# Fused attention, channel mix and gated feed-forward on one core: four more heads without a split, wider first loads, and new planner numbers

## The chip, the cores and the metric

The kernel runs on one NeuronCore of a Trainium2 chip. The metric is device time in microseconds (us) of one execution; lower is better. Engines go by short names: PE is TensorE (PEld its weight loads), DVE is VectorE, ACT is ScalarE, POOL is GpSimd, SP is SyncE, which issues nearly all the DMA transfers here.

## The reference

Three blocks follow each other in float32 on a batch of 4 with 576 positions: block-causal attention (8 heads of 64), a channel mix with a feed-forward (512 to 1024 to 512), and a gated feed-forward with a product over positions.

```python
scores = scale * np.matmul(q, k.transpose(0, 1, 3, 2))
mask = (pos[:, None] // 64) >= (pos[None, :] // 64)
attn = softmax(np.where(mask, scores, -1e9))
x = (attn @ v)                      # heads side by side: (4, 576, 512)

xk = mu_k * x + (1.0 - mu_k) * x_prev        # x_prev: one position earlier
xr = mu_r * x + (1.0 - mu_r) * x_prev
k = np.maximum(xk @ w_k, 0.0)
x = sigmoid(xr @ w_r) * (k * k @ w_v)

h = gelu(x @ w_in); u, v = split(h)
v_s = einsum('ts,bsd->btd', w_sg, layernorm(v) * g_ln) + b_sg
out = x + (u * v_s) @ w_out
```

## The kernel before

**Two ways to multiply in float32.** PE multiplies plain float32 in two passes at half the column rate of the type `float32r`, which holds fewer digits. Most products are therefore made of pairs: an operand is split into a high part and the rest (`xh`/`xl`, `kh`/`kl`, `PH`/`PL`, `K`/`k2`), and two or three `float32r` products are added up in PSUM. The split costs work on ACT (the rounding copy), POOL and DVE (the subtraction). A direct product takes plain float32 and needs no split.

**Attention.** The unit of work is one batch, one head and one kind: `LO` has the queries 0 to 319, `HI` the queries 320 to 575 with all 576 keys. There are 64 units; the first 16 are `LO` of batches 0 and 1, the next 16 `HI` of the same batches. Units with a number under `DIRECT = 16` are direct: their q and k come by one transfer of 66 rows (64 of the head, two that carry the mask) into `t[0:66]`, their v by another. A unit makes scores (`emit_S`, into the PSUM tiles `SA`, `SB`, or `M` for two early ones), the row maxima on DVE (`stats`), exponentials on ACT (`P`), transposes on PE (`emit_T`, into `T`), a copy of these out of PSUM (`PH` or `PL` for direct units, both for split ones), and the product with v (`emit_PV`, `direct_PV`, into `O`). A direct unit's output stands with the queries as rows, and PE transposes it once more for each pair of heads (`otmp`).

**Feed-forwards.** From the first four pairs of heads on, the mixed inputs (`mix`, tiles `t`, `xh`, `xl`) go into products of 288 columns with the weights, in PSUM tile `M`. The weights come as float64 words and are turned into `float32r` pairs by a chain over ACT, DVE and POOL (`w_split`, tiles `u`, `th`, `w`). The later attention units are spread between these products. The gated feed-forward of all four batches follows from about 440 us on.

**The planner.** The kernel first records every operation, and `Plan.play` then plays them through a table of costs and latencies: the next operation on an engine is the ripe one with the least rank. The order so found is written out as the program. `takes` holds the costs, `Gate` a model of PE's clock with two levels, `MB`, `CB`, `XV` and others shift ranks. Where the planner sees PE stand still it writes fillers, which multiply a tile of zeros (`calm`): 128 columns wide, or, while an output in `O` is open, zeros added into that output (`zeros`). A filler changes no result.

## Time and profile before

| | |
|---|---|
| median of 3 runs | 702.46 us (701.78 to 705.37) |
| profiled execution | 702.29 us |
| its span, first to last instruction | 700.6 us |
| PE busy, share of the span | 691.2 us, 99% |
| DVE, ACT, POOL busy | 467.8, 462.7, 326.9 us (67%, 66%, 47%) |

The span lies inside the execution's own time; 1.7 us of it are outside. Busy time of PE counts overlapping matmuls as one stretch, so that 99% doesn't mean that PE works at its peak. All of the kernel's operations go through one helper, so that every row has the same source line (L586, in the change L596), and the tiles tell the rows apart.

### The profile page before, as it was taken

To read this page: it belongs to the slowest core of one execution; us is meant where nothing else is said; L and a number is where in the kernel's file an instruction comes from. 1 tells how busy PE (TensorE), PEld (TensorE's weight loads), DVE (VectorE), ACT (ScalarE), POOL (GpSimd) and SP (SyncE) were. 2 spreads that over 40 slices of the span, in tenths; PEclk is the share of its full clock that TensorE was granted. 3 is DMA by queue.
4 is the path that set the end of the run, shared out by engine and by line. 5 is a ranking of instruction groups with operands and counts; after the bars stand their busy time and mean duration, and the time that the engine had idled before them with its cause. 6 is when DMAs were issued, how large, how long until landed. Compare 5 with 4: busy or idle time off the path is not lost.

```text
span 700.6 us, 13886 instructions
## 1 busy us (share of the span) xinstructions
PE 691.2 (99%) x4953; PEld 661.9 (94%) x4953; DVE 467.8 (67%) x1169; ACT 462.7 (66%) x1301; POOL 326.9 (47%) x386
## 2 busy tenths in 40 slices
PE   8999999999999999999999999999999999999998
PEld 7888899998999999999999999999899998998998
DVE  3887656877877776775777886773899256346223
ACT  5767898898899899899799889682552132032120
POOL 4634657566566667567557654340334032022031
PEclk9999999999999999999999999999999999999999
DMA  8852126423322332433323310721900400400102
GB/s 256 345 143 64 36 69 197 139 76 110 102 70 84 109 105 68 140 90 111 104 85 96 111 59 16 251 78 52 356 14 1 137 1 0 136 1 9 61 1 68
DMA packets 34565, 69.21 MB, mean 99 GB/s; under 512 B 6048, under 2 KB 20384, under 8 KB 34496
## 3 DMA queue, kind: packets, MB, share of 16 engines
q1 hardware_dynamic: 34352, 68.32, 30.7%
q8 instruction: 39, 0.64, 0.4%
q14 instruction: 30, 0.25, 0.1%
q10 hardware_dynamic: 144, 0.00, 0.0%
HBM read 55.47 MB, written 9.44 MB: 93 GB/s over the span
## 4 chain that ended last, share of the span: by engine, by line
PE 87%; ACT 7%; DVE 2%; DMA 2%; issue 1%; POOL 1%; ACTq 0%; POOLq 0%
PE M L586 43%; PE O L586 17%; PE T L586 11%; PE V L586 7%; PE SA L586 5%; PE SB L586 5%; ACT P L586 2%; DMA q<-Q 1%; ACT PH L586 1%; ACT R L586 1%; ACT otmp L586 1%; ACT t L586 1%; ACT K L586 0%; ACT kh L586 0%; ACT Q L586 0%
## 5 line engine op out<-in xcount | busy, mean ns | idle before, releaser
L586 PE MATMUL M<-xh,w 128*128 128x288 f32 x688 | 163.6, 305 | 0.6 <-ACT xh L586 0.3
L586 PEld LDWEIGHTS M<-xh,w 128*128 128x128 f32 x688 | 117.5, 189 | 1.8 <-ACT xh L586 0.6
L586 PE MATMUL M<-xl,w 128*128 128x288 f32 x344 | 102.5, 299 | 0.0
L586 PE MATMUL M<-kh,w 128*128 128x288 f32 x416 | 97.7, 302 | 0.0
L586 PE MATMUL T<-ident,P 128*128 128x128 f32 x480 | 79.0, 287 | 1.3 <-ACT P L586 0.6
L586 POOL TENSOR_TENSOR gt<-gt,U 128x288 f32<-128x288 f32 x32 | 30.2, 946 | 102.4 <-DVE gt L586 51.4
L586 POOL TENSOR_TENSOR xl<-t,xh 128x288 fp32r<-128x288 f32 x64 | 53.7, 839 | 50.1 <-ACT xh L586 50.0
L586 DVE TENSOR_TENSOR PL<-T,PH 128x256 fp32r<-128x256 f32 (+3 forms) x128 | 68.4, 545 | 11.7 <-ACT PH L586 10.2
L586 ACT ACTIVATE PH<-T 128x384 fp32r<-128x384 f32 (+4 forms) x144 | 65.8, 480 | 9.1 <-PE T L586 8.5
L586 PEld LDWEIGHTS M<-kh,w 128*128 128x128 f32 x416 | 70.6, 188 | 0.0
L586 PEld LDWEIGHTS T<-ident,P 128*128 128x128 f32 x480 | 61.1, 149 | 6.5 <-DVE PL L586 1.9
L586 POOL TENSOR_TENSOR kl<-R,kh 128x288 fp32r<-128x288 f32 x64 | 54.0, 848 | 27.1 <-ACT kh L586 24.8
L586 PEld LDWEIGHTS M<-xl,w 128*128 128x128 f32 x344 | 65.1, 189 | 0.1
L586 DVE TENSOR_SCALAR_CACHE_REDUCE P<-P,rr 128x448 f32<-128x448 f32 (+3 forms) x112 | 63.9, 594 | 0.9
L586 POOL TENSOR_TENSOR k<-qkv,K 64x576 fp32r<-64x576 f32 (+1 forms) x48 | 60.3, 1256 | 5.0 <-ACT K L586 2.3
L586 PE MATMUL M<-kl,w 128*128 128x288 f32 x208 | 61.6, 296 | 0.0
L586 ACT ACTIVATE U<-M 128x288 f32<-128x288 f32 x32 | 13.2, 411 | 71.8 <-PE M L586 71.8
L586 POOL TENSOR_TENSOR V<-qkv,V 128x320 fp32r<-128x320 f32 (+1 forms) x48 | 38.1, 793 | 32.7 <-ACT V L586 22.3
L586 POOL TENSOR_TENSOR Q<-qkv,Q 64x256 fp32r<-64x256 f32 (+1 forms) x48 | 37.9, 790 | 32.1 <-PE SB L586 12.0
L586 PE MATMUL O<-gh,w 128*128 128x288 f32 x256 | 52.0, 295 | 0.1
L586 PE MATMUL O<-PL,V 128*128 128x256 f32 (+2 forms) x208 | 51.6, 284 | 0.3 <-DVE PL L586 0.3
L586 PE MATMUL O<-PH,V 128*128 128x256 f32 (+2 forms) x208 | 51.9, 279 | 0.0
(186 smaller groups left out, 1938.3 us busy)
## 6 DMA issues: line engine op xcount, KB each, us to landing
qkv<-qkv_hi_dram SPq DMA_DIRECT2D x32, 576.0 KB, 3.8
qkv<-qkv_lo_dram SPq DMA_DIRECT2D x16, 416.0 KB, 3.6
x2d<-th SPq DMA_DIRECT2D x32, 144.0 KB, 2.9
X<-x2d SPq DMA_DIRECT2D x4, 1152.0 KB
outT_dram<-o SPq DMA_DIRECT2D x32, 144.0 KB, 1.8
w<-w_k_dram SPq DMA_DIRECT2D x8, 512.0 KB, 7.7
w<-w_v_dram SPq DMA_DIRECT2D x8, 512.0 KB, 9.0
w<-w_in_dram SPq DMA_DIRECT2D x8, 512.0 KB, 8.3
```

What stands on the lines that cost most here:

```text
L586: getattr(getattr(self.nc, e), fn)(*pos, **{k: real(x) for k, x in a.items() if k[0] != "_"})
```

## The change

`DIRECT` goes from 16 to 20: units 16 to 19, the first four `HI` units (heads 0 to 3 of batch 0), become direct, with q, k and mask rows from a new input `later`. The inputs `first` and `later` get 128 rows of which the last 62 are zeros, and the first `PADDED = 4` units load and multiply all 128. The transfer of v loses 64 columns of zeros. In the planner, transposes and products get other costs, a matmul may not start before its weights could be loaded behind the matmul ahead (`preload`, `began`), and seven constants change.

```diff
-BACKLOG = 8000
+BACKLOG = 6000
-FILL_DUTY = 0.7
+FILL_DUTY = 1.0
+COOL = 0.44
...
-            self.slow = u < (HOT if self.slow else 0.38)
+            self.slow = u < (HOT if self.slow else COOL)
...
+def preload(fn, a):
+
+    if fn == "transpose":
+        return 100.0
+    return (220.0 if a["lhsT"].tile.dt == F32 else 109.0) * (1.0 if a["lhsT"].cols > 64 else 0.51)
...
                     gap = t - free[e]
+                    s = t = max(t, began + preload(op.alts[i][1], op.alts[i][2]) * (2.0 if gate.slow else 1.0))
...
-MB = 0
-CB = -500
+MB = -300
+CB = -200
...
-DIRECT = 16
+DIRECT = 20
+PADDED = 4
...
-            nc.sync.dma_start(out=t[0:66, 0:nq + nk], in_=first[b, h])
-            nc.sync.dma_start(out=t[:, nq + nk:nq + nk + nv + 64], in_=src[:, nq + nk:nq + nk + nv + 64])
-            splits[n] = (t[0:66, 0:nq], t[0:66, nq:nq + nk], None)
-            vs[n] = t[:, nq + nk:nq + nk + nv + 64]
+            r = 128 if n < PADDED else 66
+            nc.sync.dma_start(out=t[0:r, 0:nq + nk], in_=(later if kind else first)[b, h, 0:r])
+            nc.sync.dma_start(out=t[:, nq + nk:nq + nk + nv], in_=src[:, nq + nk:nq + nk + nv])
+            splits[n] = (t[0:r, 0:nq], t[0:r, nq:nq + nk], None)
+            vs[n] = t[:, nq + nk:nq + nk + nv]
...
-        for c in CHUNKS[LO]:
+        pe(sum(c + 1 for c in CHUNKS[kind]) * 220.0)
+        chunks = CHUNKS[kind]
+        N = len(chunks)
+        for i, c in enumerate(chunks):
             for j in range(c + 1):
-                u, src = next((u, o) for u, (ts, _) in enumerate(GROUPS[LO]) for tj, tc, o in ts if (tj, tc) == (j, c))
-                mm(ot[:, 64 * c:64 * c + 64], trans[n, u][0][:, src:src + 128], V[:, 64 * j:64 * j + 64],
+                u, src = next((u, o) for u, (ts, _) in enumerate(GROUPS[kind]) for tj, tc, o in ts if (tj, tc) == (j, c))
+                mm(ot[:, 64 * i:64 * i + 64], trans[n, u][0][:, src:src + 128], V[:, 64 * j:64 * j + 64],
                    start=j == 0, stop=j == c)
...
+    def direct(q0, q1, *blocks):
+
+
+        qk = np.concatenate([i[n][0:2].swapaxes(2, 3)[..., lo:q1] for n, lo in (("q", q0), ("k", 0))], axis=-1)
+        rows = np.zeros_like(qk)
         for r, s in enumerate(blocks):
-            rows[..., r, s:s + 64] = 1.0
-            rows[..., r, q1 + s + 64:q1 + s + 128] = -2.0 ** 33
+            rows[..., r, s - q0:s - q0 + 64] = 1.0
+            rows[..., r, q1 - q0 + s + 64:q1 - q0 + s + 128] = -2.0 ** 33
         return c(np.concatenate([qk, rows], axis=-2))
...
+        "first": direct(0, 320, 64, 192),
+        "later": direct(320, S, 320, 448),
```

How the change moves instructions is shown at three places. The first is the start of PE's program, with the scores of units 0 to 2 and the transposes of unit 0. The tiles `kh` and `kl` hold the loads of the first four units at this point (two in each). Before:

```order
L586 MATMUL O<-calm 64x128 x15
L586 MATMUL SA<-kh 64x64
L586 MATMUL SA<-kh 128x192
L586 MATMUL SB<-kh 128x320
L586 MATMUL M<-kh 64x64
L586 MATMUL M<-kh 128x192
L586 MATMUL M<-kh 128x320
L586 MATMUL T_159<-ident,P_88 128x128 x3
L586 MATMUL T_170<-ident,P_88 128x128 x3
L586 MATMUL SB<-kl 64x64
L586 MATMUL SB<-kl 128x192
L586 MATMUL SA<-kl 128x320
```

With the change:

```order
L596 MATMUL O<-calm 64x128 x18
L596 MATMUL SA<-kh 64x64
L596 MATMUL SA<-kh 128x192
L596 MATMUL SB<-kh 128x320
L596 MATMUL M<-kh 64x64
L596 MATMUL M<-kh 128x192
L596 MATMUL M<-kh 128x320
L596 MATMUL SB<-kl 64x64
L596 MATMUL SB<-kl 128x192
L596 MATMUL T_165<-ident,P_88 128x128 x2
L596 MATMUL T_173<-ident,P_88 128x128
L596 MATMUL SA<-kl 128x320
```

Two pieces of the third unit's scores now stand ahead of the first unit's transposes, and three fillers are added.

The second place is DVE at the same time: row maxima (`stats`), the first outputs (`otmp`) and the weight chain (`u`, `th`). Before:

```order
L586 TENSOR_REDUCE stats<-SA 128x1
L586 TENSOR_SCALAR u<-u 128x512
L586 TENSOR_REDUCE rr<-sums 128x3
L586 TENSOR_SCALAR u<-u 128x512
L586 TENSOR_TENSOR otmp<-O,rr 128x3x64
L586 SCALAR_TENSOR_TENSOR u<-w,u 128x512
L586 RECIPROCAL rr<-rr 128x3
L586 SCALAR_TENSOR_TENSOR u<-w,u 128x512
L586 TENSOR_SCALAR u<-u 128x512
L586 TENSOR_REDUCE stats<-M 64x1
L586 TENSOR_SCALAR u<-u 128x512
L586 TENSOR_REDUCE stats<-M 128x1 x2
```

With the change:

```order
L596 TENSOR_REDUCE stats<-SA 128x1
L596 TENSOR_REDUCE stats<-M 64x1
L596 TENSOR_REDUCE stats<-M 128x1
L596 TENSOR_REDUCE rr<-sums 128x3
L596 RECIPROCAL rr<-rr 128x3
L596 TENSOR_TENSOR otmp<-O,rr 128x3x64
L596 TENSOR_REDUCE rr<-sums 128x3
L596 RECIPROCAL rr<-rr 128x3
L596 TENSOR_REDUCE stats<-M 128x1
L596 TENSOR_SCALAR u<-u 128x512 x2
L596 TENSOR_TENSOR otmp<-O,rr 128x3x64
L596 SCALAR_TENSOR_TENSOR u<-w,u 128x512
```

The maxima of the fourth unit (`stats<-M`) now come ahead of the whole weight chain; ahead of them stood two of its steps `u<-w,u` and four `u<-u`, now none.

The third place is one `HI` unit on PE, its product with v and the next unit's scores. Before, split (the letters `k`, `q` are the second pair):

```order
L586 MATMUL O<-PH_1374,V 128x256
L586 MATMUL O<-PL_1384,V 128x256
L586 MATMUL SA<-K,Q 128x448
L586 MATMUL SA<-k_145,q_161 128x448
L586 MATMUL O<-PH_1378,V 128x256
L586 MATMUL O<-PL_1397,V 128x256
L586 MATMUL O<-PH_1378,V 128x256
L586 MATMUL O<-PL_1397,V 128x256
L586 MATMUL O<-PH_1404,V 128x128
```

With the change, direct:

```order
L596 MATMUL O<-calm 64x128 x8
L596 MATMUL O<-qkv,PH_1443 128x64
L596 MATMUL O<-qkv,PH_1478 128x64 x2
L596 MATMUL O<-qkv,PH_1495 128x64
L596 MATMUL O<-qkv,PH_1443 128x64
L596 MATMUL O<-qkv,PH_1478 128x64 x2
L596 MATMUL O<-qkv,PH_1495 128x64
L596 MATMUL SA<-qkv 128x448
L596 MATMUL M<-kh,w 128x288
L596 MATMUL M<-kl,w 128x288
```

Ten `float32r` products of up to 256 columns with v become nine plain ones of 64 columns, and six pieces of scores become three plain ones.

## Rows read from the trace of the kernel before

**Rows 1.** The page: busy time of PE, and its granted clock in 40 slices.

```profile
PE 691.2 (99%) x4953; PEld 661.9 (94%) x4953; DVE 467.8 (67%) x1169; ACT 462.7 (66%) x1301; POOL 326.9 (47%) x386
...
PEclk9999999999999999999999999999999999999999
```

**Rows 2.** Busy time by stage: window, length, engines, PEclk, DMA share, GB/s.

```profile
0.00:49.00 49.00, 47.24 (x192) 39.65 (x192) 34.28 (x86) 32.08 (x93) 24.04 (x41) 1.00 0.76 254
49.00:76.50 27.50, 26.07 (x216) 22.09 (x216) 20.61 (x58) 19.14 (x59) 11.11 (x10) 1.00 0.24 74
76.50:130.00 53.50, 52.86 (x391) 49.70 (x391) 33.82 (x88) 47.59 (x146) 36.30 (x37) 1.00 0.37 109
76.50:440.00 363.50, 360.61 (x2770) 352.12 (x2770) 265.18 (x726) 328.63 (x980) 230.74 (x267) 1.00 0.32 95
```

**Rows 3.** Timeline of PE ahead of 50 us: start, length, engine, tiles, form, number.

```profile
1.18 1.86 PE L586 MATMUL O<-calm 128*64 128x128 f32 x15 [1.18 <-POOL calm L586]
3.62 1.42 PE L586 MATMUL SA<-kh 66*64 66x64 f32 x4 [0.57 <-DMA kh<-first_dram]
...
36.30 1.27 PE L586 MATMUL SA<-qkv 66*128 66x320 f32 x2
37.37 0.85 PE L586 MATMUL T<-ident,P 128*128 128x128 f32 x3
...
42.08 2.67 PE L586 MATMUL O<-qkv,PH 128*128 128x64 f32 x12
44.54 0.85 PE L586 MATMUL T<-ident,P 128*128 128x128 f32 x3
...
47.94 2.00 PE L586 MATMUL O<-qkv,PL 128*128 128x64 f32 x12
```

**Rows 4.** The same view behind 57 us.

```profile
60.49 0.85 PE L586 MATMUL SB<-qkv 66*64 66x64 f32 x4
61.18 0.70 PE L586 MATMUL SA<-qkv 66*128 66x320 f32 x2
61.72 0.28 PE L586 MATMUL T<-ident,P 128*128 128x128 f32 x1
...
76.48 0.38 PE L586 MATMUL M<-xh,w 128*128 128x288 f32 x1
...
85.38 1.45 PE L586 MATMUL O<-qkv,PH 128*128 128x64 f32 x12
86.64 0.38 PE L586 MATMUL M<-xh,w 128*128 128x288 f32 x1
```

**Rows 5.** The same view of split HI units: transposes, scores, product with v.

```profile
141.45 0.82 PE L586 MATMUL T<-ident,P 128*128 128x128 f32 x6
...
144.16 0.37 PE L586 MATMUL SA<-K,Q 128*128 128x448 f32 x1
...
145.09 0.30 PE L586 MATMUL M<-xh,w 128*128 128x288 f32 x1
...
145.90 0.28 PE L586 MATMUL O<-PH,V 128*128 128x256 f32 x1
...
147.08 0.29 PE L586 MATMUL M<-xh,w 128*128 128x288 f32 x1
```

**Rows 6.** Busy time by window: fillers (calm) alone, then all up to unit 10's maxima.

```profile
49.00:76.50 27.50, 5.75 (x77) 5.15 (x77) 0.00 (x0) 0.00 (x0) 1.00 0.24 74
...
0.00:69.25 69.25, 66.52 (x360) 56.19 (x361) 49.34 (x127) 45.31 (x134) 32.31 (x48) 1.00 0.62 204
```

**Rows 7.** Groups of 100 to 440 us: busy us, mean ns of one, idle before.

```profile
L586 ACT ACTIVATE K<-qkv 128x576 fp32r<-128x576 f32 x32 | 21.7, 679 | 0.0
...
L586 ACT ACTIVATE V<-qkv 128x320 fp32r<-128x320 f32 x32 | 15.0, 470 | 0.1
...
L586 ACT ACTIVATE Q<-qkv 128x256 fp32r<-128x256 f32 x32 | 13.3, 417 | 3.1 <-PE SB L586 2.8
...
L586 ACT ACTIVATE otmp<-O 64x256 f32<-64x256 f32 x32 | 12.1, 379 | 3.1 <-PE O L586 2.0
```

## The prediction

> **What bounds the kernel now.** I read the page first: PE is busy for 99% of the span [rows 1], and its matmul row overlaps, so this says only that PE never waits long. The windows by stage then tell three stretches apart [rows 2]. Up to 49 us PE is busy for 47.2 us with 192 matmuls; from 49 to 76.5 us 216 matmuls fit into 27.5 us. Behind that the matmul row is full to 99% (360.6 of 363.5 us up to 440 us) and the weight-load row idles for 11.4 us, while ACT is at 89% (47.6 of 53.5 us) just behind 76.5 us. So the long part is bound by PE's own work, with ACT close behind it.

> The timeline shows what is odd about the start. Twelve records `O<-qkv,PH` take from 42.08 to 44.54, 0.205 us each [rows 3]; the same twelve take from 85.38 to 86.64, 0.105 us each [rows 4]. Two records of 66x320 scores take 1.07 us (36.30 to 37.37) [rows 3] and later 0.54 us (61.18 to 61.72) [rows 4]. [...] The column of the granted clock says 1.00 throughout [rows 1, 2]; the durations contradict it ahead of 48 us, and I go by them. What PE did just before: from 44.54 to 47.94 it ran transposes and products of all 128 rows only, whereas until then scores of 66 rows stood in between [rows 3]. Scores and transposes of 66 and 128 rows from 3.62 us on did not raise the clock.

> **The change part by part.** As a mark I take the first of the twelve products of the third weight block, which starts at 76.48 us [rows 4]. PE's program up to there can be counted in both kernels.

> *Prices at full pace.* A direct product with v is two records, 0.21 us; a transpose is 0.105 us (six start within the 0.58 us from 141.45 to 142.03, and the last overlaps with what follows) [rows 5]; the scores of a direct LO unit are 0.69 us (60.49 to 61.18) and 0.54 us [rows 4], 1.23 us; a 288-column product is 0.13 us, at the rate of the split scores (2,048 columns in the 0.93 us from 144.16 to 145.09 [rows 5]); a filler of 128 columns is 0.075 us (77 in 5.75 us [rows 6]).

> *Before, up to the mark:* 66 products with v (13.9), 81 transposes (8.5), 13 starts and 12 ends of scores (15.5), 24 products (3.2): 41.1 us of work. Besides 15 fillers at the lower pace (1.6, [rows 3]) and 77 (5.8), 1.2 us of start, 0.8 us until the first load, and half of the 45 us spent at the lower pace, 22.4. That is 72.9; 3.6 us are waits that no filler covers.

> *With the change, up to the mark:* 54 products with v (11.3), 71 transposes (7.5), 11 units of scores (13.5), 24 products (3.2): 35.5 us. Fillers: 18 at the lower pace (1.9), 100 of 128 columns (7.5), and 23 of a kind that before lacks, zeros added to an open output in plain float32. Those cost between a filler (0.075) and a direct product, whose shape and type they have (0.21); I take 0.21, as they load the same weights: 4.8 us, lower end 1.7. Start and first load: 2.1, as 128 rows in place of 66 move twice the bytes and three more fillers cover part of it.

> *The clock.* Scores of units 0, 1 and part of 2 now stand back to back with 128 rows. By the rows this is the kind of stretch that went ahead of the rise at 48 us, and it lasts from about 4 to 9.5 us. I take the rise at 9.5 us: 5.5 us at half pace, 2.8 us lost in place of 22.4. Bounds: it can't rise before PE starts (0), and it may rise as late as the first run of 288-column products (a rival, below).

> *Waits at the new pace.* At double pace PE meets the other engines earlier. Up to unit 10's maxima (69.25 us) ACT was busy for 45.3 us and DVE for 49.3 [rows 6]. The order now puts 39 in place of 58 steps of the weight chain on DVE ahead of these maxima (some 9 us less), and on ACT 21 in place of 30, for which a few mixing steps come in (some 3 us less). ACT then needs 42 us of a mark at about 56: 75%, less than the 89% that it held behind 76.5 us. So it can keep up, and I put 2 us for waits; 0 below, 6 above.

> The mark comes at 35.5 + 14.2 + 2.1 + 2.8 + 2.0 = 56.6 us, 20 us earlier. DMA doesn't hold it: in 0 to 49 us the queues are busy for 0.76 [rows 2], the first four loads grow by 163 KB each, and every direct load of v shrinks by 32 KB.

> *Given back behind the mark.* First, work that stood ahead of the mark now stands behind it: 12 products, 10 transposes, two units' scores, 5.5 us. Second, the four HI units. Split, one costs 0.93 us for scores and 1.18 us for the product with v (145.90 to 147.08) [rows 5], 2.11 us. Direct, 1,024 columns at 0.54 us for 320 give 1.73 us, nine products 1.89 us, and one extra transpose per unit 0.10: 3.72 us. That is 1.6 us more each, 6.4 us in all. Since PE is full there, it is on the path; only waits could hide it (the weight-load row idles for 3.8 us from 76.5 to 130 us [rows 2]), so 3 to 6.4. Third, fillers behind the mark: 13 become 18 of 128 columns and 4 of the dearer kind, 1.2 us more.

> *Relief.* Each of the four units drops `Q`, `K`, `V` and `otmp` on ACT (0.42 + 0.68 + 0.47 + 0.38 us [rows 7]), 1.95 us, and adds half an `xT` copy of about 0.4 us; POOL and DVE lose their subtractions. The waits that this can remove are part of the 11.4 us in which no weights load up to 440 us [rows 2]. I take 1.5 us for relief and better order together; 0 to 8.

> *Planner numbers* (`BACKLOG`, `COOL`, ranks, costs) act by the order alone, and that is counted above, apart from latencies, which are part of the waits.

> Sum: the execution's own 702.3 (span 700.6 and 1.7 outside) - 19.9 + 5.5 + 6.4 + 1.2 - 1.5 = 694.0 us. The profiled execution is 0.2 us from the median of before, so no correction is due.

> [...] The nine transposes from 44.54 to 47.94 us took more of that stretch than the five products of 288 columns, and the clock rose right behind [rows 3]. [...]

> **The rivals.**
> 1. *Early rise, but ACT and DVE hold PE.* If ACT runs only at the 65% that it had up to 69.25 us (45.3 of 69.25 [rows 6]), its 42 us put the mark at 65 us: 8.4 us later, 702.4 us, no change. For it: chains of maxima, exponentials and copies are as long as before, and the 49 to 76.5 us stretch at full pace had ACT at 70% only [rows 2]. Against it: that order was made for other latencies.
> 2. *The clock rises late: slower.* If plain float32 scores of 128 rows aren't enough, and the first 288-column products are needed, which now stand about 40 rows down the program, the rise comes at some 30 us or the pace falls back after it. Between 9.5 and 30 us half of 20.5 us is lost, 10.3 us, and fillers at half pace add more: 704 to 710 us. It decides against the change once the mark is later than about 65 us, for 13.1 us of work stand against it less 1.5 of relief.
> 3. *More goes than I count:* the waits up to 440 us shrink by 8 us in place of 1.5, or the dearer fillers cost as little as the others: 684 to 688 us. For it: ACT's load falls by some 7 us there.
> 4. *The four units cost nothing or the padding does nothing:* the latter alone is rival 2; the former is held off by PE being full.

> **How the numbers follow.** Forecast (688.5 to 698.5): 0.65. Rival 1 (699 to 704): 0.14. Rival 2 (704 to 711): 0.09. Rival 3 (683 to 688): 0.12. About 0.5%, 3.5 us, is what a measurement of this kernel tells from no change. Faster by more, under 699.0: 0.65 + 0.12 + a sliver of rival 1, 0.78. Within 0.5%: the rest of rival 1 and the lowest part of rival 2, 0.14. Slower: 0.08. The range of 685 to 703 leaves out rival 2 and a part of rival 3.

> **What would show it.** The twelve records of the first `O<-kh,PL` take 1.3 us rather than 2.5, and the rise lies at about 10 us; a later one shows at once in scores of 320 columns that still take 0.53 us a record. The third weight block starts at 52 to 60 us. ACT's share up to there is 70 to 85%. In the four HI units scores of 128x448 take 0.37 us a record and eighteen `O<-qkv` records 1.9 us. The new fillers `O<-calm` of 64 columns stand 0.105 us apart. From the mark to the end the time is 633 to 637 us, against 624.1 before. I am wrong if the clock falls back between 10 and 50 us, if the mark comes later than 62 us with ACT under 70%, or if the stretch behind the mark grows by much more than 12 us.

## The result and the profile after

The changed kernel takes 694.26 us (median of four runs, 693.84 to 694.6) against 702.59 us for the kernel before beside it: a ratio of 0.9874, 95% interval 0.9846 to 0.9902. The forecast was 694.0 us.

The page of the changed kernel (busy time, share of the span, instructions), and of its last part the engines' shares of the chain of work that ended last:

```profile
span 691.9 us, 14054 instructions
PE 684.7 (99%) x5074; PEld 658.2 (95%) x5074; DVE 450.8 (65%) x1141; ACT 453.8 (66%) x1287; POOL 308.6 (45%) x374
...
PE 95%; DVE 2%; ACT 2%; DMA 0%; issue 0%; POOL 0%; POOLq 0%; ACTq 0%
```

The timeline of PE (start, length, engine, tiles, form, number of records, and in brackets the wait before it with its releaser). The length of a group overlaps with what follows, so a record's pace is read from the start of a group to the start of the next:

```profile
3.78 1.41 PE L596 MATMUL SA<-kh 128*64 128x64 f32 x4 [0.42 <-DMA kh<-first_dram]
4.99 1.27 PE L596 MATMUL SB<-kh 128*128 128x320 f32 x2
6.19 1.90 PE L596 MATMUL M<-kh 128*64 128x64 f32 x6
...
9.03 0.70 PE L596 MATMUL SA<-kl 128*128 128x320 f32 x2
9.58 0.55 PE L596 MATMUL T<-ident,P 128*128 128x128 f32 x3
...
11.19 1.45 PE L596 MATMUL O<-kh,PL 128*128 128x64 f32 x12
12.47 0.83 PE L596 MATMUL T<-ident,P 128*128 128x128 f32 x6
...
19.05 1.90 PE L596 MATMUL O<-calm 128*128 128x64 f32 x16
20.75 0.52 PE L596 MATMUL M<-xh,w 128*128 128x288 f32 x2
...
57.74 0.54 PE L596 MATMUL M<-xh,w 128*128 128x288 f32 x1
...
134.68 2.12 PE L596 MATMUL O<-qkv,PL 128*128 128x64 f32 x18
136.61 0.38 PE L596 MATMUL M<-xh,w 128*128 128x288 f32 x1
```

Two records of 320-column scores take 1.20 us from 4.99 and 0.55 us from 9.03. In between PE went from half pace to full pace; the trace also records when the granted clock changes, and its first such record, a granted clock of 1.0, lies at 7.4 us. Twelve records of `O<-kh,PL` take 1.28 us, as twelve took at full pace before [rows 4]. The third weight block, the mark of the prediction, starts at 57.74 us in place of 76.48.

The windows up to the mark and behind it (window, length, PE, PEld, DVE, ACT, POOL, granted clock, DMA share, GB/s), and the fillers alone up to the mark:

```profile
0.00:57.74 57.74, 54.83 (x434) 47.21 (x434) 36.49 (x103) 40.96 (x128) 22.91 (x44) 1.00 0.69 229
57.74:130.00 72.26, 72.26 (x528) 66.67 (x527) 47.81 (x112) 57.55 (x170) 36.21 (x37) 1.00 0.25 79
...
0.00:57.74 57.74, 16.58 (x164) 14.90 (x164) 0.21 (x1) 0.21 (x1) 1.00 0.69 229
```

PE stands still for only 2.9 us up to the mark (57.74 less 54.83), ACT is busy for 71% of it. From the mark to the end it is 691.9 - 57.74 = 634.2 us, where before had 624.1 [rows 2, 4].

### The profile page after: what moved, and what is told of

It is laid out like the page before. It is cut to its first block, busy times and chain, and to the rows that moved or that the text cites. A ratio compares the mean times of both kernels' runs of the same rounds, so it can differ in the third digit from the quotient of the medians.

```text
span 691.9 us, 14054 instructions
## 1 busy us (share of the span) xinstructions
PE 684.7 (99%) x5074; PEld 658.2 (95%) x5074; DVE 450.8 (65%) x1141; ACT 453.8 (66%) x1287; POOL 308.6 (45%) x374
## 4 chain that ended last, share of the span: by engine, by line
PE 95%; DVE 2%; ACT 2%; DMA 0%; issue 0%; POOL 0%; POOLq 0%; ACTq 0%
PE M L596 49%; PE O L596 19%; PE T L596 10%; PE V L596 7%; PE SB L596 5%; PE SA L596 5%; ACT P L596 1%; DVE th L596 1%; DMA kh<-first_dram 0%; DVE stats L596 0%; DVE u L596 0%; ACT PH L596 0%; DVE otmp L596 0%; ACT otmp L596 0%; DVE o L596 0%
## 5 line engine op out<-in xcount | busy, mean ns | idle before, releaser
L596 PE MATMUL M<-xh,w 128*128 128x288 f32 x704 | 166.8, 305 | 0.1
L596 PE MATMUL M<-kh,w 128*128 128x288 f32 x432 | 104.0, 307 | 0.0
L596 PE MATMUL T<-ident,P 128*128 128x128 f32 x480 | 74.3, 274 | 0.3 <-ACT P L596 0.3
L596 DVE TENSOR_TENSOR PL<-T,PH 128x320 fp32r<-128x320 f32 (+3 forms) x116 | 61.8, 543 | 17.4 <-ACT PH L596 16.5
L596 POOL TENSOR_TENSOR kl<-R,kh 128x288 fp32r<-128x288 f32 x64 | 53.6, 840 | 32.4 <-ACT kh L596 31.3
L596 PEld LDWEIGHTS T<-ident,P 128*128 128x128 f32 x480 | 58.0, 141 | 3.1 <-ACT P L596 0.8
L596 DVE TENSOR_SCALAR_CACHE_REDUCE P<-P,rr 128x448 f32<-128x448 f32 (+3 forms) x104 | 58.2, 582 | 0.6
L596 POOL TENSOR_TENSOR k<-qkv,K 64x576 fp32r<-64x576 f32 (+1 forms) x44 | 53.7, 1221 | 4.4 <-ACT K L596 2.3
L596 PE MATMUL M<-XHL,w 128*128 128x288 f32 x384 | 51.7, 294 | 0.0
L596 PEld LDWEIGHTS M<-XHL,w 128*128 128x128 f32 x384 | 51.2, 188 | 0.1
L596 PE MATMUL O<-PH,V 128*128 128x256 f32 (+2 forms) x188 | 47.3, 279 | 0.0
```

The lines of the kernel that those rows point to most:

```text
L596: getattr(getattr(self.nc, e), fn)(*pos, **{k: real(x) for k, x in a.items() if k[0] != "_"})
```

## The experiments

Theory A, which the expectations name, is the prediction's account: scores of 128 rows raise the clock early, and this gains nearly all, less what four direct `HI` units cost PE. The rivals are told with each. Every ratio is to the kernel before, with its 95% interval; every diff is against the changed kernel unless it says otherwise. The planner orders each variant anew, so that its order changes too, except in `same_order_66`, `no_fill`, `no_zero_fill` and `pad_plan_light`, which keep an order. All variants keep the shorter transfer of v, so no run prices that alone.

**One part alone.** `pad_only` is the kernel before with the wider loads and scores of units 0 to 3:

```diff
 (kernel before)
+PADDED = 4
+            r = 128 if n < PADDED else 66
```

> Of the three parts only the padding is kept: 128 rows for units 0 to 3, units 16 to 19 split as before, the old planner numbers (and the shorter v load). Theory A (the padding raises the clock early, and the four direct HI units cost about 5 us): the rise at 7 to 10 us, the third weight block at 55 to 62 us, the whole at 687 to 693 us, thus faster than the full change. Theory B (the gain is the new order, the padding matters little): 699 to 704 us.

Measured: 703.63 us, 1.0001 (0.9975 to 1.0027). The clock rose at 7.6 us, as theory A says, but the mark came only at 75.9 us, and nothing was gained: of theory A only the rise held, its 687 to 693 us did not. The early clock alone is worth nothing; the experiment `old_ranks` below bears on why.

`plan_only` has the planner's new numbers (the costs of ACT and POOL steps among them) and 66 rows throughout:

```diff
-DIRECT = 20
-PADDED = 4
+DIRECT = 16
+PADDED = 0
```

> Only the planner numbers are new: 66 rows in all direct loads, units 16 to 19 split. Theory A: the clock rises later than 25 us and the whole takes 698 to 705 us. Theory B: 690 to 696 us.

Measured: 701.39 us, 0.9943 (0.9908 to 0.9978). Its PE timeline shows the pace going up and down again:

```profile
52.85 0.29 PE L596 MATMUL M<-xh,w 128*128 128x288 f32 x1
53.07 0.85 PE L596 MATMUL SA<-qkv 66*64 66x64 f32 x4
53.62 0.43 PE L596 MATMUL M<-xl,w 128*128 128x288 f32 x1
53.90 0.29 PE L596 MATMUL M<-xh,w 128*128 128x288 f32 x1
56.31 1.58 PE L596 MATMUL T<-ident,P 128*128 128x128 f32 x6 [2.12 <-ACT P L596]
57.68 1.27 PE L596 MATMUL SB<-qkv 66*128 66x320 f32 x2
```

Four records of 64 columns take 0.55 us at 53.07. PE then waits 2.12 us for exponentials on ACT, and the scores at 57.68 take 0.53 us a record, half pace. The clock records say full from 50.1 to 56.9 us and again from 74.0.

`direct_only` makes units 16 to 19 direct in the kernel before:

```diff
 (kernel before)
-DIRECT = 16
+DIRECT = 20
```

> Only units 16 to 19 are made direct: 66 rows, old planner numbers. Theory A: PE is full where these units stand, so 1.6 us each less some relief: 705 to 710 us. The rival, that relief of ACT, DVE and POOL is worth more than PE's added work: 695 to 701 us.

Measured: 711.28 us, 1.0078 (1.0042 to 1.0115); the clock rose at 61.2 us, the mark came at 82.8. Alone it is a loss, and more than its 6.4 us on PE. Of the 9.4 us between the profiled spans (710.0 against 700.6) 6.3 lie ahead of the mark, since here the planner made another start as well.

**Two parts together.** `direct_plan` leaves out only the padding:

```diff
-PADDED = 4
+PADDED = 0
```

> Direct HI units and planner numbers without the padding, planned anew for 66 rows. Theory A: 703 to 710 us, the rise later than 25 us. Theory B (the order brings the gain): 692 to 697 us.

Measured: 709.18 us, 1.0058 (1.002 to 1.0095). Full pace from 50.7 to 57.5 us, then half until 78.0; the mark at 74.1. Against the whole change that is 15 us, the size that the prediction gave to the early clock (20, of which 5 come back as work behind the mark). Against `plan_only`, which splits the four units, the direct units cost 7.8 us here (709.18 against 701.39): in these two orders they relieve nothing.

`pad_plan` leaves out only the direct `HI` units:

```diff
-DIRECT = 20
+DIRECT = 16
```

> Padding and planner numbers, but units 16 to 19 split as before. Theory A: 3 to 6 us less than the full change, 688 to 691 us. The rival, that the direct HI units pay for themselves by relief: 695 us or more.

Measured: 709.5 us, 1.0073 (1.0048 to 1.0099). Here theory A fell: the start is as good as with the whole change (clock at 11.0 us, mark at 59.2), yet without the four direct units, which cost PE 1.6 us each, the kernel is 15 us slower, and 8 us slower than `plan_only`, which lacks only the padding. The loss lies behind the mark. Windows of 100 to 150 us of this kernel, all work first, then the fillers alone (PE first):

```profile
100.00:150.00 50.00, 44.53 (x369) 37.97 (x369) 42.10 (x105) 43.28 (x121) 37.50 (x38) 1.00 0.44 137
...
100.00:150.00 50.00, 13.22 (x156) 11.78 (x156) 0.00 (x0) 0.00 (x0) 1.00 0.44 137
```

The same of the changed kernel:

```profile
100.00:150.00 50.00, 50.00 (x378) 47.64 (x378) 25.81 (x61) 38.67 (x105) 27.36 (x29) 1.00 0.34 109
...
100.00:150.00 50.00, 1.30 (x13) 1.13 (x12) 0.00 (x0) 0.00 (x0) 1.00 0.34 109
```

PE's real work in these 50 us is 31.3 us without the direct units (44.53 less 13.22) and 48.7 with them. Each of the three helpers (DVE, ACT, POOL) is busier without them. PE's waits in `pad_plan` from 95 to 165 us name DVE (engine, tile waited for, releaser: us in total, times, longest):

```profile
PE T L596 <- DVE PL L596: 2.2, 2, 1.3
PE O L596 <- DVE xT L596: 1.6, 3, 0.7
PE O L596 <- DVE otmp L596: 0.5, 1, 0.5
```

What is missing on PE shows in the windows of the records that write tile `M`, which here are nearly all products of the channel mix. First `pad_plan`:

```profile
100.00:150.00 50.00, 5.42 (x27) 1.00 0.44 137
150.00:165.00 15.00, 15.00 (x113) 1.00 0.18 62
```

Then the changed kernel:

```profile
100.00:150.00 50.00, 30.83 (x193) 1.00 0.34 109
150.00:165.00 15.00, 8.80 (x57) 1.00 0.29 96
```

In `pad_plan` nine split units stand together in 100 to 150 us (nine `SA<-K,Q`, the first at 102.11) with 27 products between them; the changed kernel has three direct and three split units there, the first split one at 132.85, and 193 products. By 165 us (from 100) `pad_plan` is 110 products short, and at 0.13 us each that is 14 us.

Split units alone don't make this loss. The kernel before has seven of them in the same window, and there PE has no filler at all (0.00 us in the window of `calm`), although ACT is busier than in `pad_plan`:

```profile
100.00:150.00 50.00, 49.53 (x380) 48.05 (x379) 34.95 (x90) 44.92 (x129) 33.77 (x35) 1.00 0.47 143
```

`plan_only`, with six, has none either:

```profile
100.00:150.00 50.00, 49.88 (x384) 48.67 (x383) 31.95 (x81) 39.44 (x118) 28.38 (x31) 1.00 0.39 121
```

So the loss belongs to the order that the planner made in `pad_plan`, not to the helpers' load as such. No run has the four units split in the order of the changed kernel, which would part the two.

**The rows or the order?** `same_order_66` has the changed kernel's order and loads, but the scores of units 0 to 3 read 66 of the 128 rows:

```diff
+            cut = (first 66 rows of the view) if n < PADDED else (the view)
-            splits[n] = (t[0:r, 0:nq], t[0:r, nq:nq + nk], None)
+            splits[n] = (cut(t[0:r, 0:nq]), cut(t[0:r, nq:nq + nk]), None)
```

> The changed kernel in its own order with the same loads, but the scores of units 0 to 3 read only the first 66 of the 128 rows. Theory A (the rows raise the clock): the rise later than 20 us, the third weight block at 65 us or later, the whole at 702 to 712 us. The rival, that the order alone brings the early rise (scores back to back, 18 fillers): 693 to 696 us.

Measured: 716.0 us (710.37 to 719.27), 1.0158 (1.0075 to 1.024); the profiled execution is the shortest of them, and the median lies above the 702 to 712 us expected. Its PE timeline:

```profile
5.04 1.27 PE L596 MATMUL SB<-kh 66*128 66x320 f32 x2
6.25 2.48 PE L596 MATMUL M<-kh 66*64 66x64 f32 x6
...
17.30 1.27 PE L596 MATMUL M<-kl 66*128 66x320 f32 x2
18.50 0.48 PE L596 MATMUL SB<-qkv 66*64 66x64 f32 x2
...
34.78 1.27 PE L596 MATMUL SB<-qkv 66*128 66x320 f32 x2
35.84 2.66 PE L596 MATMUL O<-kl,PH 128*128 128x64 f32 x12
```

The 320-column scores still take 0.53 us a record at 34.78; full pace comes at 44.1 us by the clock records, the mark at 73.9. Not one instruction stands elsewhere, so the 62 rows of zeros themselves move the rise from 44.1 to 7.4 us and the mark by 16 us, about what parts the two profiled executions (710.37 against 693.84 us). All fourteen traces agree: in the nine kernels with scores of 128 rows the rise lies between 7.4 and 13.1 us, in the five with 66 rows between 44.1 and 61.2 us.

**The fillers.** `no_fill` keeps the order but writes only the first 18 fillers; `no_zero_fill` leaves out the 27 that add zeros to an open output:

```diff
 (no_fill)
+            if op.n < 0:
+                fills += 1
+                if fills > 18:
+                    continue
 (no_zero_fill)
+            if op.n < 0 and op is not self.filler:
+                continue
```

> The changed kernel in its own order, but of its fillers only the first 18 are written out. Theory A: fillers stand in waits; the time is 691 to 695 us as long as the clock stays up. The rival, that fillers hold the clock up: it falls back between 10 and 50 us and the time is 698 us or more. A third reading, that the fillers delay PE: under 690 us.

> The changed kernel in its own order without the 27 fillers that add zeros to an open output (54 records at 0.105 us, 5.7 us of PE). If they stand in waits: within 1 us of the full change, 693 to 695 us. If they delay PE: 689 to 692 us.

Measured: `no_fill` 699.24 us, 0.9954 (0.9939 to 0.9968); `no_zero_fill` 697.26 us, 0.9896 (0.9826 to 0.9965), an interval that does not part it from the whole change, though all four executions (694.71 to 698.65) are longer than each of the changed kernel's (693.84 to 694.6). Windows of `no_fill`:

```profile
0.00:30.00 30.00, 25.75 (x154) 20.09 (x155) 17.41 (x52) 20.09 (x65) 11.98 (x35) 1.00 0.78 259
...
34.00:41.00 7.00, 5.74 (x41) 4.75 (x40) 4.00 (x11) 5.45 (x17) 2.56 (x3) 0.95 0.64 209
41.00:65.00 24.00, 23.06 (x86) 18.82 (x86) 15.28 (x40) 15.40 (x46) 8.96 (x8) 0.51 0.57 191
```

The rise is there (10.8 us), but the clock falls at 31.3, comes back at 34.7 and stays low from 41.5 to 65.4 us. Ahead of the second fall PE worked for 5.74 of 7 us; the changed kernel, with fillers in its waits, works for 39.07 of the 40 us from 20 to 60 and never falls. The mark comes at 62.5 us. `no_zero_fill` loses the pace as well, from 31.6 to 41.8 us by its clock records, and its mark comes at 60.2 us:

```profile
34.00:41.00 7.00, 6.90 (x44) 6.23 (x44) 3.24 (x8) 3.73 (x12) 1.07 (x2) 0.50 0.59 200
```

Its expectation, 693 to 695 us if these fillers stand in waits and 689 to 692 if they delay PE, left out that they hold the pace too. The fillers are not free. PE reaches the fifth product with `xh` at 30.66 us in `no_fill` and at 30.18 in `no_zero_fill`, ahead of both falls, against 31.87 with all fillers. They delay PE there by 1.2 to 1.7 us, but they hold the pace, and the balance is 5.0 us in their favour for all of them and about 3 for the zero-adding ones.

**How many direct units?** `direct_18` and `direct_24` change the one number:

```diff
-DIRECT = 20
+DIRECT = 18   (and 24)
```

> The changed kernel with two direct HI units instead of four. If DVE and POOL are what holds PE behind 100 us once the start is short, and each direct HI unit takes load off them: between the full change and the run with none, 697 to 706 us. If the run with none was an unlucky order and a direct HI unit only costs 1.6 us of PE: 690 to 693 us.

> The changed kernel with eight direct HI units instead of four. The full change has few waits left behind 80 us, so that four more units should cost their price on PE, 1.6 us each less some relief: 697 to 701 us. If relief goes on to pay: 690 to 694 us.

Measured: two direct `HI` units 695.11 us, 0.9896 (0.9867 to 0.9925), not parted from four by these intervals; eight 701.49 us, 0.9983 (0.9969 to 0.9997). From four to eight the profiled span grows from 691.9 to 698.8 us, 1.7 us for each unit, the price that the prediction put on PE (1.6). Neither range expected for two units held (697 to 706, or 690 to 693 us), and eight came out just above the 697 to 701 named. In `direct_18` PE's real work from 100 to 150 us is 41.4 us, between the 31.3 of none and the 48.7 of four.

**The ranks.** `old_ranks` is the whole change with the two rank shifts of before:

```diff
-MB = -300
-CB = -200
+MB = 0
+CB = -500
```

> The changed kernel with only the two ranks as before: MB 0 and CB -500, which puts the weight chain ahead of the heads' own steps on DVE. If the ranks are what lets PE use the early rise: the third weight block at 65 us or later and 700 to 708 us. If the costs and latencies do it: 692 to 697 us.

Measured: 708.2 us, 1.0078 (1.0053 to 1.0104). The clock rises at 10.1 us, but the mark comes at 80.5, 22.8 us later than in the changed kernel; behind it 8.6 us come back. Windows of PE's products with `xh` (the first input of the channel mix) show what PE lacks. First `old_ranks`:

```profile
20.00:40.00 20.00, 1.19 (x4) 1.00 0.48 162
40.00:60.00 20.00, 1.07 (x4) 1.00 0.62 210
60.00:80.00 20.00, 2.04 (x8) 1.00 0.31 96
```

Then the changed kernel:

```profile
20.00:40.00 20.00, 2.29 (x8) 1.00 0.53 189
40.00:60.00 20.00, 4.83 (x18) 1.00 0.68 226
60.00:80.00 20.00, 10.73 (x47) 1.00 0.18 57
```

16 products against 73 up to 80 us. The mixing steps that make `xh` stand behind the weight chain: from 20 to 80 us DVE does 34 steps on `u` and 4 steps `t<-xT` with the old ranks, 25 and 8 with the new. PE fills the gap: all work and the fillers alone in 20 to 80 us with the old ranks,

```profile
20.00:80.00 60.00, 56.76 (x527) 50.98 (x528) 42.83 (x114) 40.81 (x122) 23.09 (x18) 1.00 0.47 156
...
20.00:80.00 60.00, 23.25 (x271) 20.92 (x271) 0.00 (x0) 0.00 (x0) 1.00 0.47 156
```

23.25 us of fillers, against 14.06 with the new ranks, while DVE is busy for 71% and ACT for 68%. `pad_only`, with the same old ranks, has 22.14 us of fillers there. This is the prediction's first rival (an early rise that the other engines hold back), and here it is true, by the order of their steps and not by their load, as neither is full.

**Is DVE's load what holds PE in `pad_plan`?** `pad_plan_light` keeps that kernel's order and leaves out, for units 16 to 23, the scaling of the exponentials by their sums, `P<-P,rr`, on DVE (and on ACT where that does it); this part of the computation is missing:

```diff
 (pad_plan, where the program is written out)
+            if 16 <= getattr(op, "n_unit", 0) < 24:
+                continue
```

> Padding and planner numbers, units 16 to 19 split, in the order of that run, but the scaling of P by the row sums on DVE is left out for units 16 to 23 (16 instructions of 0.60 and 0.73 us, 10.7 us of DVE in all; part of the computation is missing). If DVE is what PE waits for between 100 and 160 us: DVE's share at 120 to 140 us falls below 0.85, fillers stay as they are in the program, and the time falls from 709.5 to 699 to 705 us. If it is POOL, ACT or the order: 707 us or more.

Measured: 709.19 us, 1.009 (1.0063 to 1.0118), no gain. All work and the fillers alone from 100 to 150 us:

```profile
100.00:150.00 50.00, 44.78 (x377) 38.76 (x376) 35.33 (x77) 43.92 (x122) 38.44 (x39) 1.00 0.45 139
...
100.00:150.00 50.00, 13.84 (x160) 12.30 (x160) 0.00 (x0) 0.00 (x0) 1.00 0.45 139
```

DVE has 6.8 us less to do (42.10 to 35.33), and PE gains nothing: 30.9 us of real work after 31.3, and it stands empty for 5.2 us after 5.5. The order and its fillers were kept, so these 5.5 us are all that could have gone in this window; the expectation of 699 to 705 us asked for more than that. In the chain of work of this stretch ACT and POOL pieces (`P`, `PH`, `Q`, `k`) take the place of DVE's. So this part of DVE's load does not alone make the waits in this order; an order planned anew without the scaling was not tried.

## Why the prediction was right, and where its steps were not

The time (694.0 against 694.26) and its two halves hold: the mark was put at 56.6 us and came at 57.7, the rest at 636 us and came at 634.2.

- **The clock** was put at 9.5 us and came at 7.4. That the rows of zeros do it, and neither the order nor the loads, is shown by `same_order_66`. The reading that led there was thinner than it says. The run from 44.54 to 47.94 us was not of 128 rows only, as three transposes of 64 rows stand in it, and from 37.37 to 44.54 us PE also ran records of 128 rows alone, at half pace (twelve of `O<-qkv,PL` from 38.01 to 40.56, 0.21 us each) and without a rise. Two lines of the kernel before that show it:

```profile
38.01 2.75 PE L586 MATMUL O<-qkv,PL 128*128 128x64 f32 x12
...
45.32 0.98 PE L586 MATMUL T<-ident,otmp 64*128 64x64 f32 x3
```

That 128 rows at the start would do was thus a guess, and a lucky one. The runs show that the rows matter, not what exactly raises the clock. The 45 us at half pace that the forecast counts in the kernel before end at 49.0 us by its first clock record.
- **Work and fillers up to the mark.** The count of filler records was right (164). A zero-adding record stands 0.106 us from the next (16 from 19.05 to 20.75), so the dearer of the two bounds, 0.21 for two, was the right choice. All fillers together are busy for 16.58 us, 2.4 more than the 14.2 taken; the row counts overlap with what follows, so the difference is an upper bound.
- **Waits.** PE is empty for 2.9 us up to the mark, of which 2.1 were put down to the start. The second rival (a late or falling clock) didn't come about, and the first not with these ranks. The loads were no hindrance; each of the first four grew by 155 KB (165 to 320), not 163. ACT's share, 71%, lies at the lower end of the 70 to 85% named.
- **Direct `HI` units on PE.** Eighteen records take 1.93 us (1.89 taken); 1.7 us more per unit in `direct_24` (1.6 taken).
- **Relief** is the step that was wrong in itself. It was put at 1.5 us, 0 to 8, as part of the waits that the kernel before has. The runs show no such constant. With the padding and the new numbers, four split units make the kernel 15 us longer than direct ones (`pad_plan`); with 6.4 us for the direct units on PE, that is some 22 us of waits and fillers avoided. Without the padding the same four direct units lose 7.8 us (`direct_plan` against `plan_only`), more than their price. The sum came out because it took the changed program's own fillers behind the mark (18 and 4) and PE as full there, and so it was: 72.26 of 72.26 us to 130 us. That the four units save no more than 1.5 us by relief was neither needed for it nor shown. Of the third rival (8 us of relief, or cheap fillers) neither half came: the rest is 1.5 us shorter than forecast, and the zero-adding fillers are the dear kind.
- **Planner numbers** were said to act by the order alone. That is so, but the prediction gave them no price, and with two of them set back the kernel is 14 us longer (`old_ranks`).

The three parts do not add up: alone they give 1.0001, 0.9943 and 1.0078, together 0.9874. The padding gains 15 us with the direct units in place (against `direct_plan`) and loses 8 without them (`pad_plan` against `plan_only`). The early clock is worth its 15 us only in an order in which PE finds work to use it on: the mix products up to 80 us (the ranks), and products between the `HI` units up to 150 us.

**Transposes.** The changed kernel holds full pace from 7.4 us to the end with 508 transposes on the way (480 `T<-ident,P` and 28 `T<-ident,otmp`, from 8.7 to 434.0 us). `no_fill`, with the same transposes but with waits in place of fillers, falls back at 31.3 and at 41.5 us, so these runs show that waits matter and can't say what a transpose does to the clock.

**What stays open.** Why the planner sets nine split units together with 27 products in `pad_plan`, and not so with two direct ones, and thus how much of the 22 us is relief and how much is one unlucky order. The runs exclude the scaling on DVE alone; ACT (87% busy there) and POOL (75%) weren't relieved one by one, and in the kernel before ACT is busier (90%) without a filler. Nor was padding with direct units but the old numbers tried.

## What to carry to other kernels

Where a faster clock comes early, look next at what PE has to do in that time: with the old planner numbers the same clock was worth nothing (703.63 us), and fillers took the place of products. Parts of a change to a planned program can't be priced one by one from the rows of before; count the new program whole, and expect the parts alone to come out quite otherwise. The same four direct units cost 8 us in one order (`direct_plan`) and gained 15 in another (against `pad_plan`); with padding and new numbers, two units gained nearly all, four hardly more, and eight gave it back. Where a variant is planned anew, a run that keeps the order, such as `same_order_66`, is what shows a cause.
